# Weight scaling moved from GpSimd to ScalarE and batch 1 to 3 logits by 32-column matmuls, in a clustered attention and rational-activation MLP kernel

## The chip, the cores and the metric

One core of one Trainium2 chip runs the whole program. The metric is device time in microseconds of that core. Engine names are those of the profile: PE is TensorE (matmuls), PEld its weight loads, DVE VectorE, ACT ScalarE, POOL GpSimd, SP the queue that issues every data transfer.

## The reference, cut to what matters

```python
# q, k, v: (4, 8, 768, 64); centroids: (8, 16, 64)
q_assign = argmax(einsum('bhsd,hcd->bhsc', q_n, c_n), -1)   # q_n, k_n, c_n: rows of length 1
k_assign = argmax(einsum('bhsd,hcd->bhsc', k_n, c_n), -1)
mask = q_assign[..., :, None] == k_assign[..., None, :]
scores = where(mask, q @ k.T / 8, -1e9)
attn = softmax(scores) @ v
x = attn.transpose(0, 2, 1, 3).reshape(3072, 512)
h = x @ w_in                                                # w_in: (512, 2048)
P = a0 + a1*h + a2*h**2 + a3*h**3
Q = 1 + |b0|*|h| + |b1|*h**2
return (P / (Q + 1e-6)) @ w_out                             # w_out: (2048, 512)
```

Each row of q and of k is given to the cluster whose centroid has the largest inner product with it, its 16 **logits**; a query sees only the keys of its own cluster.

## The kernel before, in words

**Number format.** Operands of the large matmuls are split into two float16 parts, a high part and a low part (value minus high part), after a multiplication by a power of two. A product is three float16 matmuls (high by high, high by low, low by high) added up in PSUM.

**Weights** (`weights`, L660). `w_in` and `w_out` come in four chunks each. A chunk is four tiles of 128 x 512 that are loaded by SP, put together from 32-bit words by ACT and DVE (L701 and L708 are two DVE steps), and summed up so that a power of two follows (`wis` and `wos`). Then, for each of two pairs of tiles: one ACT operation over 1024 elements writes the high part as `scale * w` (the `act` call at L760; all ACT operations have the helper's line L546 in the profile); for each of the two tiles POOL multiplies the float32 words by the power of two in place (`tensor_scalar`, L777) and subtracts the high part from them, which gives the low part (`tensor_tensor`, L784). That is 16 ACT operations, 32 POOL multiplications and 32 POOL subtractions in all. The float32 words lie in a ring of 8 buffers (`big`) that raw loads and the MLP's intermediates use too.

**Attention.** Work goes by batch (4) and pair of heads (4 a batch). `prep` (L943) loads a pair's q, k and v, scales and splits them, turns them by transposing DMAs (PE in two pairs of batch 0), and then computes the logits of the pair's 2 x 768 queries and 2 x 768 keys into one tile `ptl` of 24 groups of 16. `logits` (L1154) does this with 48 matmuls (L1158), two for each group: the high part of the centroids starts a group's sum and their low part ends it, both with the same stationary operand and 16 columns. DVE takes the largest of each group (L1189), marks where it is reached (L1190, into `df`), and DVE and POOL make a mask of it that is appended to q and k before they are turned. Batch 0 then runs `attend_keys` (L1377); batches 1 to 3 run `attend` (L1255): 144 times, scores by four matmuls of 384 columns (L1277), minimum and scale on DVE (L1292), exponential and high part on ACT, low part on DVE (L1312), a transposing DMA, and the product with v (L1331).

**MLP** (`moe`, L1581). 12 blocks of 256 tokens: `x @ w_in` into tiles `ph` (L1639), the rational function on ACT, DVE and POOL, and the product with `w_out` into `po` (L1750).

**PSUM.** Eight banks in three rings: `m`, two single banks (`NM = 2`, used by `ph`, the attention outputs `px`, `ptl` and small things); `s`, two tiles of two banks each (the score tiles of `attend`); `o`, one tile of two banks (`po`).

**Order.** Every operation of every engine stands in a list written out by hand (`ORDER`, L31): 1001 entries for ACT, 1165 for DVE, 861 for PE, 640 for POOL, 384 for SP. A planner reads the lists, gives out buffers of the rings in that order and emits the program; semaphores follow from the data. An engine runs its list in sequence, so an entry that waits holds up all that stand behind it.

Of the kernel before, what the change touches and what calls it, by code (L numbers as in the profile page):

```python
# [27 lines left out]
K = {'ghd': 0.0, 'rvp': 0, 'look': 62.89, 'mulp': 0.4, 'sub': 0, 'xn': 14, 'NR': 8, 'sgp': 1, 'scp': 1, 'vsc': 0.75, 'sup0': 0, 'stk': 2, 'lop': 0, 'mgp': 0, 'rvn': 2, 'tq2': 2, 'at': 3, 'es': 4, 'vn': 2, 'ah': 5, 'rel': 0, 'twin': 1, 'pet': '_01', 'avs': 3, 'ksum': 1, 'fst': '_0', 'hpa': 1}  # L28
# [348 lines left out]
def clustered_attention_moe_kernel(  # L377
# [282 lines left out]
    def weights(name, i, vt):  # L660
# [91 lines left out]
        for m in range(2):  # L752
            hl = [whl[name, i, 2 * m + d] for d in range(2)]

            def hi(m=m):
                if name == "wi":
                    return win[i][:, 0, 2 * m : 2 * m + 2]
                return wout[i][:, 0, 2 * m : 2 * m + 2]

            act(  # L760
                ac(1024, 1), hi, lambda m=m: wp[m].ap.bitcast(F32), AF.Identity, [ws[2 * m], ws[2 * m + 1], ws_], hl, vt, [wp[m]],
                scale=sc,
            )
# [1105 lines left out]
```

## Time and profile before

| | |
|---|---|
| median of 3 runs | 896.92 us (894.39 to 898.39) |
| profiled execution, time | 897.27 us |
| profiled execution, span | 895.4 us |
| mean granted clock of PE | 0.994 |
| batch 0 attention and weights | about 0 to 205 us of the span |
| attention of batches 1 to 3 beside the MLP | about 179 to 760 us |
| MLP of the last batch alone | about 760 to 895 us |

Sums below are made against the profiled execution's 897.27 us; 1.9 us of it lie outside the span. The engines work side by side, so a busy time is not a share of the whole that could be added up with another's. A group of instructions has its busy time, the mean of one in ns, and behind the bar's end the idle time of its engine just before it and who ended that. PE's matmuls overlap in the records: two that start 25 ns apart are both shown with 169 ns.

### The profile page before, as it was taken

The page shows a single profiled execution, that of the slowest core. Times are in us where ns is not written, and L with a number is a line of the kernel's source. Part 1 is how long each engine was busy: PE and PEld are TensorE (multiplying, and loading weights), DVE is VectorE, ACT ScalarE, POOL GpSimd, SP SyncE. Part 2 cuts the span into 40 slices and gives each one's busy share as a digit, 9 for nine tenths or more (in the row PEclk, how much of TensorE's full clock was granted, in tenths as well). Part 3 has the DMA queues.
Part 4 walks back from the last instruction along what each step waited for, and adds up shares of the span by engine and source line. Part 5 has one row for each costly group of instructions (what it writes and reads, how often), then busy time and mean ns, then how long its engine had stood idle before and what let it go on. Part 6 is the DMA issues. An engine that isn't in the chain of part 4 may idle for free.

```text
span 895.4 us, 22725 instructions
## 1 busy us (share of the span) xinstructions
PE 849.1 (95%) x9045; PEld 597.8 (67%) x9045; DVE 785.8 (88%) x1388; ACT 755.2 (84%) x1050; POOL 629.3 (70%) x661
## 2 busy tenths in 40 slices
PE   2789999898999999999999999999999999999998
PEld 2557666675766777567776767777677666766664
DVE  7998979689989899999989998999889888876786
ACT  7557786899999989988999999998988898766674
POOL 1354685699988898778898988789988877422331
PEclk9899999999999999999999999999999999999999
DMA  8478755747989889999999799969888866300000
GB/s 278 138 170 198 190 161 144 206 96 145 194 166 217 159 163 213 188 191 197 167 220 175 154 186 179 180 133 214 144 159 126 160 126 113 87 1 25 7 25 25
DMA packets 364395, 134.70 MB, mean 150 GB/s; under 512 B 342144, under 2 KB 358528, under 8 KB 364288
## 3 DMA queue, kind: packets, MB, share of 16 engines
q1 hardware_dynamic: 364288, 133.24, 73.7%
q8 instruction: 71, 1.16, 0.5%
q14 instruction: 36, 0.29, 0.1%
HBM read 41.98 MB, written 6.29 MB: 54 GB/s over the span
## 4 chain that ended last, share of the span: by engine, by line
PE 55%; DVE 16%; ACT 11%; DMA 6%; issue 5%; POOL 5%; SPq 0%; ACTq 0%; DVEq 0%; POOLq 0%
PE po L1750 19%; PE ph L1639 17%; PE s L1277 6%; PE px L1331 5%; DVE top L1435 3%; ACT s L546 3%; DVE s L1292 3%; ACT u L546 2%; PE px L1506 2%; DVE ah L1312 2%; ACT ah L546 2%; PE z L1487 2%; DVE s L1732 1%; PE s L1408 1%; DMA rwi<-in_moe_w_in_dram 1%
## 5 line engine op out<-in xcount | busy, mean ns | idle before, releaser
L1639 PE MATMUL ph<-x,win 128*128 128x256 f16 x2304 | 267.6, 273 | 2.8 <-DVE xf L1357 1.2
L1750 PE MATMUL po<-wout,u 128*128 128x512 f16 x1152 | 268.6, 379 | 0.0
L1639 PEld LDWEIGHTS <-win 128*128 128x128 f16 x2304 | 223.2, 98 | 43.2 <-DVE xf L1357 3.5
L1679 POOL TENSOR_TENSOR s<-s,u 128x512 f32<-128x512 f32 x96 | 129.0, 1362 | 94.2 <-issue 52.6
L1750 PEld LDWEIGHTS <-u 128*128 128x128 f16 x1152 | 110.5, 98 | 115.3 <-issue 0.5
L1312 DVE SCALAR_TENSOR_TENSOR ah<-s,ah 128x768 f16<-128x768 f32 x144 | 136.1, 952 | 23.7 <-ACT ah L546 22.5
L1292 DVE TENSOR_SCALAR_CACHE_REDUCE s<-s,cc 128x768 f32<-128x768 f32 x144 | 145.2, 1019 | 9.3 <-PE s L1277 8.8
L546 ACT ACTIVATE s<-s,nm 128x768 f32<-128x768 f32 x144 | 125.4, 873 | 21.2 <-DVE s L1292 19.0
L1277 PE MATMUL s<-sk,sq 128*128 128x384 f16 x576 | 116.5, 329 | 4.1 <-DVE ah L1312 3.4
L546 ACT ACTIVATE ah<-s 128x768 f16<-128x768 f32 x144 | 115.9, 810 | 3.1
L1702 POOL TENSOR_TENSOR s<-s,u 128x512 f32<-128x512 f32 x72 | 102.0, 1429 | 16.9 <-ACT u L546 16.5
L1739 POOL TENSOR_TENSOR u<-s,u 128x512 f16<-128x512 f32 x72 | 86.4, 1207 | 30.9 <-DVE s L1732 14.5
L1331 PEld LDWEIGHTS <-at 128*128 128x128 f16 x2592 | 88.5, 98 | 13.6 <-issue 2.2
L1331 PE MATMUL px<-vhi,at 128*128 128x65 f16 x1728 | 91.1, 194 | 1.3 <-DMA at<-ah 0.8
L1331 PE MATMUL px<-vlo,at 128*128 128x64 f16 x864 | 86.8, 192 | 0.0
L1277 PEld LDWEIGHTS <-sq 128*128 128x128 f16 x576 | 52.9, 98 | 41.6 <-DVE ah L1312 8.7
L1660 DVE TENSOR_TENSOR t<-ph,t 128x512 f32<-128x512 f32 x96 | 65.4, 684 | 12.2 <-ACT t L546 11.7
L546 ACT ACTIVATE u<-ph 128x512 f32<-128x512 f32 x96 | 56.9, 595 | 21.8 <-PE ph L1639 21.3
L1732 DVE SCALAR_TENSOR_TENSOR s<-s,t 128x1024 f32<-128x1024 f32 (+1 forms) x49 | 63.0, 1286 | 1.4 <-POOL t L1716 0.6
L546 ACT ACTIVATE u<-t 128x1024 f16<-128x1024 f32 (+1 forms) x49 | 50.9, 1039 | 11.0 <-DVE t L1722 6.0
L546 ACT ACTIVATE t<-ph,gk 128x512 f32<-128x512 f32 x72 | 55.3, 774 | 0.0
L1665 DVE SCALAR_TENSOR_TENSOR t<-t,gk,ph 128x512 f32<-128x512 f32 x72 | 53.0, 742 | 1.1
(219 smaller groups left out, 1466.6 us busy)
## 6 DMA issues: line engine op xcount, KB each, us to landing
rwi<-in_moe_w_in_dram SPq DMA_DIRECT2D x16, 512.0 KB, 4.9
rwo<-in_moe_w_out_dram SPq DMA_DIRECT2D x16, 512.0 KB, 4.8
rk<-in_k_dram SPq DMA_DIRECT2D x32, 192.0 KB, 3.5
rq<-in_q_dram SPq DMA_DIRECT2D x32, 192.0 KB, 3.6
rvm<-in_v_dram SPq DMA_DIRECT2D x16, 384.0 KB, 4.1
rv<-in_v_dram SPq DMA_DIRECT2D x16, 384.0 KB, 4.6
out_dram<-ob SPq DMA_DIRECT2D x11, 512.0 KB, 3.8
at<-ah SPq DMA_TRANSPOSE x144, 4.1
```

The costliest lines, as they stand in the source:

```text
L546: lambda: nc.scalar.activation(out=out(), in_=in_(), func=func, **{a: (x() if callable(x) else x) for a, x in kw.items()}),
L1277: nc.tensor.matmul(sc.ap[:, i, :SH], lhsT=st["q" + x].ap[:, j, t, :], rhs=st["k" + x].ap[:, j, ks, :].rearrange("p t c -> p (t c)"), start ...
L1292: lambda nm=nm, view=view: ts(out=view(), in0=view(), scalar1=cc.ap, scalar2=None, op0=ALU.mult, op1=ALU.min, accum_out=nm.ap),
L1312: lambda part=part, view=view: stt(out=part(1), in0=view(), scalar=A_SCALE, in1=part(0), op0=ALU.mult, op1=ALU.subtract),
L1331: nc.tensor.matmul(px.ap[:, i, :w_], lhsT=at.ap[:, p_, kt, :], rhs=vv.ap[:, j, kt, :w_], start=(kt == 0 and vv is vhi and p_ == 0), stop=( ...
L1639: nc.tensor.matmul(ph[i].ap[:, fi * TW : (fi + 1) * TW], lhsT=win[f // 4][:, wpart, c, f % 4 * P : (f % 4 + 1) * P], rhs=xs[c].ap[:, xpart ...
L1660: lambda i=i, th=th, ph=ph: tt(out=th[i].ap, in0=ph[i].ap, in1=th[i].ap, op=ALU.mult),
L1679: lambda i=i, sh=sh, uh=uh: nc.gpsimd.tensor_tensor(out=sh[i].ap, in0=sh[i].ap, in1=uh[i].ap, op=ALU.mult),
L1702: lambda i=i, sh=sh, uh=uh: nc.gpsimd.tensor_tensor(out=sh[i].ap, in0=sh[i].ap, in1=uh[i].ap, op=ALU.mult),
L1732: lambda tw=tw, sw=sw: stt(out=sw(), in0=sw(), scalar=2.0, in1=tw(), op0=ALU.subtract, op1=ALU.mult),
L1739: lambda i=i, sh=sh, gl=gl, g16=g16, e=(nc.vector if gld else nc.gpsimd): e.tensor_tensor(out=gl[i].ap, in0=sh[i].ap, in1=g16()[:, 0, i * ...
L1750: nc.tensor.matmul(po[ti].ap, lhsT=g16()[:, part, c0 : c0 + P], rhs=wout[f // 4][:, wpart, f % 4], start=(k == 0 and f == f_first), stop=( ...
```

## The change

Three things. In `weights`, ACT multiplies the float32 words of a pair of tiles by the power of two in place (a new operation over 1024 elements), the high part is then a copy without a scale, and POOL's multiplications are not issued any more. In `prep` for batches 1 to 3, `ptl` is a two-bank tile of the ring `s` and not a single bank of `m`; a matmul takes both parts of the centroids as 32 columns, so that 24 matmuls write the two parts of each logit beside each other; an ACT copy takes the second part into `df` as float16, and a DVE addition puts the sum into PSUM, from where L1189 and L1190 read as before. Batch 0 keeps the 48 matmuls. `ORDER` is written anew for the new set of operations: 1029 entries for ACT, 1177 for DVE, 861 for PE, 608 for POOL, 384 for SP; in its lists most operations stand within a few places of where they stood. An option `lgw` that was off is removed. The helpers that the diff calls are in the kernel above; `K` gains `'lgb': '123', 'wsa': 1`.

```diff
...
@@ -757,9 +757,15 @@
                     return win[i][:, 0, 2 * m : 2 * m + 2]
                 return wout[i][:, 0, 2 * m : 2 * m + 2]
 
+            scaled = share("wsa", ((name == "wo") + 2 * i) * 2 + m)
+            if scaled:
+                act(
+                    ac(1024, 1), lambda m=m: wp[m].ap.bitcast(F32), lambda m=m: wp[m].ap.bitcast(F32), AF.Identity, [ws_],
+                    [ws[2 * m], ws[2 * m + 1]], vt, [wp[m]], scale=sc,
+                )
             act(
-                ac(1024, 1), hi, lambda m=m: wp[m].ap.bitcast(F32), AF.Identity, [ws[2 * m], ws[2 * m + 1], ws_], hl, vt, [wp[m]],
-                scale=sc,
+                ac(1024, not scaled), hi, lambda m=m: wp[m].ap.bitcast(F32), AF.Identity, [ws[2 * m], ws[2 * m + 1], ws_], hl, vt, [wp[m]],
+                **({} if scaled else {"scale": sc}),
             )
             for d in range(2):
                 c = 2 * m + d
@@ -772,13 +778,14 @@
                         [ws[c], ws_], [hl[d]], vt, [wp[m], ptok[m]], lock=True,
                     )
                 else:
-                    op(
-                        "POOL", pt1(512, 1),
-                        lambda c=c: nc.gpsimd.tensor_scalar(
-                            out=wf(c), in0=wf(c), scalar1=sc(), scalar2=0.0, op0=ALU.mult, op1=ALU.add
-                        ),
-                        [ws_], [ws[c]], vt, [wp[m]],
-                    )
+                    if not scaled:
+                        op(
+                            "POOL", pt1(512, 1),
+                            lambda c=c: nc.gpsimd.tensor_scalar(
+                                out=wf(c), in0=wf(c), scalar1=sc(), scalar2=0.0, op0=ALU.mult, op1=ALU.add
+                            ),
+                            [ws_], [ws[c]], vt, [wp[m]],
+                        )
                     op(
                         "POOL", pt2(512, True),
                         lambda c=c, h=hl[d]: nc.gpsimd.tensor_tensor(out=h.ap[:, 1], in0=wf(c), in1=h.ap[:, 0], op=ALU.subtract),
@@ -1137,23 +1144,31 @@
             turn(x, vt + kc("p2", b, 2), by_pe)
 
         G = 4 * NT
-        wide_ = bool(kn("lgw", 0))
-        ptl = misc([P, G, NCL], F32, f"ptl{n}") if not wide_ else None
-        if wide_:
-            halves = [misc([P, G // 2, 2, NCL], F32, f"ptl{x}{n}") for x in "qk"]
-
-            def wide_logits(i):
-                x = ("q1", "k1")[i]
-                for g in range(2):
-                    for t in range(NT):
-                        nc.tensor.matmul(
-                            halves[i].ap[:, g * NT + t], lhsT=st[x].ap[:, g, t, :], rhs=cen.ap[:, 0 : 2 + i : 1 + i, h0 + g, :],
-                            start=True, stop=True,
-                        )
+        paired = str(b) in kn("lgb", "")
+        if paired:
+            ptl = bank([P, 2, 512], F32, "s", f"ptl{n}", 2)
+        else:
+            ptl = misc([P, G, NCL], F32, f"ptl{n}")
+
+        def parts(i):
+            return ptl.ap[:, :, : G * NCL].rearrange("p x (g s c) -> p x g s c", s=2, c=NCL)[:, :, :, i]
+
+        def sums_():
+            return parts(0) if paired else ptl.ap.rearrange("p (x g) c -> p x g c", x=2)
+
+        def over_rows(a):
+            return a.rearrange("p (x g) c -> p x g c", x=2)
 
         def logits():
             for g, (x, part) in enumerate((("q1", 1), ("q1", 1), ("k1", 2), ("k1", 2))):
                 for t in range(NT):
+                    if paired:
+                        nc.tensor.matmul(
+                            ptl.ap[:, g // 2, (g % 2 * NT + t) * 2 * NCL : (g % 2 * NT + t + 1) * 2 * NCL].rearrange("p (s c) -> p s c", s=2),
+                            lhsT=st[x].ap[:, g % 2, t, :], rhs=cen.ap[:, 0 : part + 1 : part, h0 + g % 2, :],
+                            start=True, stop=True,
+                        )
+                        continue
                     for i in (0, part):
                         nc.tensor.matmul(
                             ptl.ap[:, g * NT + t, :], lhsT=st[x].ap[:, g % 2, t, :], rhs=cen.ap[:, i, h0 + g % 2, :],
@@ -1163,31 +1178,18 @@
         mx, mx2 = buf([P, G], F32, "mx", f"mx{n}", 1), buf([P, G], BF16, "mxi", f"mxi{n}", 1)
         df = buf([P, G, NCL], BF16, "df", f"df{n}", 1)
         oh = df
-        if wide_:
-            ptl = buf([P, G, NCL], F32, "lsm", f"lsm{n}", 1)
-            for i, x in enumerate(("q1", "k1")):
-                op("PE", 610, lambda i=i: wide_logits(i), [cen, st[x]], [halves[i]], vt + kc("p25", b, 2.5), [df, ptl], chain="logits" + x)
-                low = buf([P, G // 2, NCL], F32, "lsl", f"lsl{x}{n}", 2)
-                act(
-                    ac(192, 0, True), lambda low=low: low.ap, lambda i=i: halves[i].ap[:, :, 1], AF.Copy, [halves[i]], [low],
-                    vt + kc("p3", b, 3),
-                )
-                op(
-                    "DVE", 290,
-                    lambda i=i, low=low: tt(
-                        out=ptl.ap[:, i * 2 * NT : (i + 1) * 2 * NT], in0=halves[i].ap[:, :, 0], in1=low.ap, op=ALU.add
-                    ),
-                    [halves[i], low], [ptl], vt + kc("p3", b, 3), co=[ptl], lock=False,
-                )
-        else:
-            op("PE", 1205, logits, [cen, st["q1"], st["k1"]], [ptl], vt + kc("p25", b, 2.5), [df], chain="logits")
+        u = vt + kc("p25", b, 2.5)
+        op("PE", 645 if paired else 1205, logits, [cen, st["q1"], st["k1"]], [ptl], u, [df], chain="logits")
+        if paired:
+            act(ac(384, 0, True), lambda: over_rows(df.ap).bitcast(F16), lambda: parts(1), AF.Copy, [ptl], [df], u)
+            dve(465, lambda: tt(out=parts(0), in0=parts(0), in1=over_rows(df.ap).bitcast(F16), op=ALU.add), [df], [ptl], u)
 
         def spread(m):
             return m.ap.unsqueeze(2).broadcast_to([P, G, NCL])
 
         u = vt + kc("p3", b, 3)
-        dve(465, lambda: nc.vector.tensor_reduce(out=mx.ap, in_=ptl.ap, axis=AX.X, op=ALU.max), [ptl], [mx], u)
-        dve(463, lambda: tt(out=df.ap, in0=ptl.ap, in1=spread(mx), op=ALU.is_ge), [ptl, mx], [df], u)
+        dve(465, lambda: nc.vector.tensor_reduce(out=mx.ap.rearrange("p (x g) -> p x g", x=2), in_=sums_(), axis=AX.X, op=ALU.max), [ptl], [mx], u)
+        dve(463, lambda: tt(out=over_rows(df.ap), in0=sums_(), in1=over_rows(spread(mx)), op=ALU.is_ge), [ptl, mx], [df], u)
         op(
             *(("DVE", 465) if fast else ("POOL", 867)),
             lambda e=(nc.vector if fast else nc.gpsimd): e.tensor_tensor(
...
```

## Rows read from the trace of the kernel before

**Rows 1.** Page part 1: busy us (share of the span) xinstructions of each engine

```profile
PE 849.1 (95%) x9045; PEld 597.8 (67%) x9045; DVE 785.8 (88%) x1388; ACT 755.2 (84%) x1050; POOL 629.3 (70%) x661
```

**Rows 2.** Windows view, four stretches: busy time of each engine (instructions)

```profile
core 0: us, PE busy (x) PEld busy (x) DVE busy (x) ACT busy (x) POOL busy (x), PEclk, DMA share, GB/s
0.00:160.00 160.00, 131.84 (x1536) 95.01 (x1537) 142.72 (x322) 113.03 (x188) 82.63 (x119) 0.98 0.67 184
160.00:205.00 45.00, 38.73 (x510) 29.40 (x510) 34.69 (x77) 43.74 (x73) 37.12 (x51) 1.00 0.61 147
205.00:280.00 75.00, 73.22 (x759) 51.38 (x759) 67.95 (x113) 69.95 (x97) 67.21 (x65) 0.98 0.91 176
280.00:760.00 480.00, 474.28 (x5254) 334.96 (x5253) 440.01 (x758) 439.83 (x588) 404.71 (x399) 1.00 0.93 170
```

**Rows 3.** Chain of waits, stretch 280 to 760: shares by engine and line

```profile
by line: PE po L1750 18.3%; PE ph L1639 17.0%; PE s L1277 9.0%; PE px L1331 7.6%; issue 6.2%; ACT s L546 4.7%; ACT u L546 3.7%; DVE s L1292 3.3%; DVE ah L1312 2.9%; ACT ah L546 2.6%; DMA sk<-tk 2.3%; POOL s L1679 2.2%; DVE s L1732 2.0%; POO
```

**Rows 4.** PE in time order around one logits pass: start us, us, what

```profile
302.52 0.75 PE L1158 MATMUL ptl<-cen,sq 128*128 128x16 f16 x24
303.12 0.75 PE L1158 MATMUL ptl<-cen,sk 128*128 128x16 f16 x24
303.72 0.38 PE L1639 MATMUL ph<-x,win 128*128 128x256 f16 x2
```

**Rows 5.** Windows view of line L1158 alone: PE and PEld busy (instructions)

```profile
160.00:205.00 45.00, 2.71 (x96) 2.55 (x96) 1.00 0.61 147
205.00:280.00 75.00, 1.35 (x48) 1.35 (x48) 0.98 0.91 176
280.00:760.00 480.00, 12.15 (x432) 11.90 (x432) 1.00 0.93 170
```

**Rows 6.** Chain of waits, whole span: one attention-times-values piece, start us, us

```profile
298.41 1.65 PE px L1331 x54
```

**Rows 7.** Groups by line and form, ACT: PSUM reads and 1024-element operations

```profile
L546 ACT ACTIVATE rs<-px 128x256 f32<-128x256 f32 x12 | 4.5, 378 | 0.2 <-PE px L1549 0.2
L546 ACT ACTIVATE u<-ph 128x512 f32<-128x512 f32 x96 | 56.9, 595 | 21.8 <-PE ph L1639 21.3
L546 ACT ACTIVATE u<-t 128x1024 f16<-128x1024 f32 x47 | 49.7, 1057 | 9.4 <-DVE t L1722 4.4 <-DVE s L1695 2.7 <-POOL s L1702 1.3
L546 ACT ACTIVATE wout<-wwo,wos 128x1024 f16<-128x1024 f32 x8 | 9.0, 1141 | 1.7 <-DVE wos L641 1.7
```

**Rows 8.** Groups by line: the second DVE read of the logits

```profile
L1190 DVE TENSOR_TENSOR df<-ptl,mx 128x384 bf16<-128x384 f32 x16 | 8.9, 555 | 0.3
```

**Rows 9.** Line L546 on ACT, 150 to 180: high parts, duration ns min/median/max, first and last start

```profile
L546 ACT ACTIVATE win<-wwi,wis x2: 1155/1156/1156, 152.7 to 153.7; 128x1024 f16<-128x1024 f32 x2
L546 ACT ACTIVATE wout<-wwo,wos x2: 1136/1142/1149, 175.1 to 178.0; 128x1024 f16<-128x1024 f32 x2
```

**Rows 10.** Windows view of line L777 alone: POOL busy (instructions)

```profile
0.00:160.00 160.00, 22.10 (x25) 0.98 0.67 184
160.00:205.00 45.00, 4.79 (x7) 1.00 0.61 147
```

**Rows 11.** Line L777 on POOL: duration ns min/median/max; then a wait

```profile
L777 POOL TENSOR_SCALAR wwi<-wwi,wis x16: 687/692/1650, 34.0 to 174.2; 128x512 f32<-128x512 f32 x16
...
  ACT win L546: 13.5, 5
```

**Rows 12.** Groups by line: one step of weight assembly on DVE, both matrices

```profile
L701 DVE SCALAR_TENSOR_TENSOR wwo<-rwo,wwo 128x512 int32<-128x512 int32 x16 | 12.9, 808 | 0.1
L701 DVE SCALAR_TENSOR_TENSOR wwi<-rwi,wwi 128x512 int32<-128x512 int32 x16 | 10.8, 686 | 0.1
```

**Rows 13.** DVE in time order: the last read of the pass in rows 4

```profile
305.19 0.56 DVE L1190 TENSOR_TENSOR df<-ptl,mx 128x384 bf16<-128x384 f32 x1
```

**Rows 14.** Line L1277 on PE (scores): what ended its idle time, us, times

```profile
  DVE ah L1312: 12.1, 22
```

**Rows 15.** Line L1639 on PE: what ended its idle time, us, times

```profile
  DVE df L1190: 1.5, 2
```

More of the change, by code (lines that the diff above doesn't have):

```diff
@@ L25 @@
 M_BIG, M_MID, M_LOW = 2.0 ** 15, 2.0 ** 7, 2.0 ** -4
-K = {'ghd': 0.0, 'rvp': 0, 'look': 62.89, 'mulp': 0.4, 'sub': 0, 'xn': 14, 'NR': 8, 'sgp': 1, 'scp': 1, 'vsc': 0.75, 'sup0': 0, 'stk': 2, 'lop': 0, 'mgp': 0, 'rvn': 2, 'tq2': 2, 'at': 3, 'es': 4, 'vn': 2, 'ah': 5, 'rel': 0, 'twin': 1, 'pet': '_01', 'avs': 3, 'ksum': 1, 'fst': '_0', 'hpa': 1}
+K = {'ghd': 0.0, 'rvp': 0, 'look': 62.89, 'mulp': 0.4, 'sub': 0, 'xn': 14, 'NR': 8, 'sgp': 1, 'scp': 1, 'vsc': 0.75, 'sup0': 0, 'stk': 2, 'lop': 0, 'mgp': 0, 'rvn': 2, 'tq2': 2, 'at': 3, 'es': 4, 'vn': 2, 'ah': 5, 'rel': 0, 'twin': 1, 'pet': '_01', 'avs': 3, 'ksum': 1, 'fst': '_0', 'hpa': 1, 'lgb': '123', 'wsa': 1}
 ORDER = {
     "ACT": """
[32 rows of a table removed]
[33 rows of a table added]
 """,
     "DVE": """
[37 rows of a table removed]
[37 rows of a table added]
 """,
     "PE": """
[28 rows of a table removed]
[28 rows of a table added]
 """,
     "POOL": """
[21 rows of a table removed]
[20 rows of a table added]
 """,
     "SP": """
[13 rows of a table removed]
[13 rows of a table added]
 """,
```

262 rows, old and new, of the table ORDER are left out of this document.

## The prediction

> **What bounds the kernel now.** I began with the page's busy shares: PE is busy for 95% of the span, DVE for 88%, ACT for 84%, POOL for 70% [rows 1]. An average over stages says little, so the next view was the windows, cut where the work changes [rows 2]. There the reader is to see three regimes. Up to 160 us (batch 0 and the weights) DVE is the fullest, with 142.7 of 160 us; PE has 28 us idle and ACT 47. From 160 to 205 us ACT is full: 43.7 of 45 us, while PE and DVE are idle for 6 and 10. From 280 to 760 us (attention of batches 1 to 3 beside the MLP) PE is idle for 5.7 of 480 us; DVE, ACT and POOL are idle for 40, 40 and 75. The last regime is the longest, so the chain of waits was read for it alone: the four large PE lines, L1750, L1639, L1277 and L1331, make 18.3 + 17.0 + 9.0 + 7.6 = 51.9% of it [rows 3]. So PE is full there, but the chain leaves it for ACT, DVE and DMA about every second microsecond: a view that bears on a rival below.
>
> **The logits matmuls.** One pass of 48 matmuls starts at 302.52 and the next PE work starts at 303.72 [rows 4]: 1.20 us, or 25.0 ns for each of 48 matmuls of 16 columns. After the change a pass has 24 of 32 columns. No row has 32 columns, so I bound one from both sides: 25.0 ns as with 16, and 1.65 us / 54 = 30.6 ns as with 64 and 65 [rows 6]. A pass then takes 0.60 to 0.73 us. I take 0.60, because 32 is nearer to 16 and the weight load that goes with each matmul stays as it is. The saving is 0.60 us a pass (0.47 at the least). The passes lie so: 432 matmuls, which is nine passes, from 280 to 760 us, one pass from 205 to 280, two from 160 to 205 [rows 5]; these are the twelve of batches 1 to 3. Where ACT is full, two passes bring nothing; from 205 us on PE is full and ten bring 10 x 0.60 = **6.0 us** (4.7 at the least price; 3.1 if only the chain's PE share counts).
>
> The Trainium skill, "TensorE: Matmul & The Clock Gate", section "Wait — 56ns, not 53.3ns?", says that matmuls never start closer than about 25 ns, and gives 25 ns for 32 columns too. By that figure a pass would be an estimated 24 x 25 = 0.60 us and the sum the same; the trace agrees for 16 columns, with 25.0 ns, and no run yet shows it for 32.
>
> **The two operations that come with them.** An ACT copy of 384 elements from PSUM lies between 378 ns (256 elements) and 595 ns (512) [rows 7]; I take the middle, 0.49 us. The DVE addition has the form of L1190, 384 elements with one input from PSUM: 0.56 us [rows 8]. For twelve pairs ACT gets 5.8 us and DVE 6.7, nine pairs of them where both are idle for 40 us each. The mask is prepared ahead of the pair that uses it, and the idle time covers them, but not wholly. In that stretch the chain's ACT pieces shown add up to 4.7 + 3.7 + 2.6 = 11.0% and the DVE ones to 3.3 + 2.9 + 2.0 = 8.2% [rows 3], so 9 x 0.49 x 0.11 + 9 x 0.56 x 0.08 = **0.9 us** is put on the path. The ends are 0 and, with the cover gone, 9 x 1.05 = 9.5 us.
>
> **The weights on ACT.** A pair of weight tiles costs ACT one operation of 1.14 us now; after it, one of that kind and one without a scale, for which the nearest row is the 1024-element ACT operation with float16 output at 1.06 us [rows 7]. That is 1.06 us more for each of 16 pairs, 17 us in all. Fourteen pairs come before 160 us, where ACT has 47 us idle and 14.8 are wanted: nothing, with up to 14.8 if the cover is gone. The last two start at 175.1 and 178.0 us [rows 9], where ACT is full: 2 x 1.06 = **2.1 us** on the path, the upper end 4.2 with the two pairs at 152.7 us that stand right ahead of the full stretch, the lower end 0 if the new lists bring other ACT work across 205 us.
>
> **The weights off POOL.** 32 multiplications go, 22.1 + 4.8 = 26.9 us busy [rows 10]. POOL is idle for 77 us before 160, so its own time counts for nothing there. What counts is DVE, the fullest: a POOL multiplication takes from 687 to 1650 ns for the same work [rows 11], 26.9 - 32 x 0.69 = 4.8 us in all above its median, so POOL and DVE hold each other up in places. On DVE's side the same step of the assembly takes 808 ns for one matrix and 686 for the other [rows 12]: 16 x 0.12 = **2.0 us** off DVE, between 0 (it was another POOL operation) and 4.8.
>
> No DMA is added or taken away, and SP's list keeps its 384 entries. What stands behind the new ACT operations is the high part and, behind it, POOL's subtraction, which must wait for both as it waits for the high part now; POOL waits for that 13.5 us in 5 places [rows 11], so the low parts can't come earlier than ACT allows.
>
> **The sum.** -6.0 + 0.9 + 2.1 - 2.0 = -5.0 us against the profiled execution's own 897.27 us: 892.3. That execution stands 0.35 us over the median of 896.92, so I say **892.0 us**.
>
> **Rivals.**
> 1. *The logits wait in the scores' place.* `ptl` now sits in one of two score tiles. Today's pass holds its bank from 302.52 to 305.19 + 0.56 = 305.75 us [rows 4, 13], 3.2 us; with 0.6 less for PE and 1.05 more for the copy and the addition it holds a score tile for 3.7 us, hand-overs not counted. PE has already waited for score tiles 22 times, 12.1 us in all [rows 14], so they are scarce. If each pass puts off the scores behind it by half its hold, twelve put them off by 22 us; PE's list has MLP work to fill this. With half of it filled 11 us stay: 892.3 + 11 = 903 us, slower. It decides once over 5/22, about a quarter, of the delay isn't filled. Against it: the rewritten lists can place MLP entries there, and the MLP's ring gets a bank back, for which PE waited only 1.5 us in 2 places [rows 15].
> 2. *PE's fullness is only apparent.* Its records overlap [rows 4]. The saving then counts by PE's share of the chain, 0.519 x 6.0 = 3.1: 897.27 - 3.1 + 0.9 + 2.1 - 2.0 = 895.2 us, no change. The Trainium skill, "Perfetto Trace Analysis", section "Identifying the Most-Contended Engine", speaks for this rival: it calls matmul busy time a bad measure and asks for the weight loads' share. By rows 2 that share is 335 of 480 us, 70%, not 98.8%. For PE speaks that the pass of rows 4 and the MLP work behind it follow each other without a gap: the saved time is time that PE's list really takes.
> 3. *ACT pays in full at the end of batch 0*, 4.2 us and no relief for DVE: 897.27 - 6.0 + 0.9 + 4.2 = 896.4 us, no change.
> 4. *Relief for DVE is at its upper end*, 4.8 us in the stretch that DVE bounds: 889.5 us.
>
> **How the numbers follow.** A measurement of this kernel can tell about 0.5%, 4.5 us, from no change. My sum gets 0.40, of which 0.28 lie more than 4.5 us below (its copies and additions are the loosest term), 0.12 within. Rival 1 gets 0.18: scarce tiles are shown, but not that PE lacks other work. Rival 2 gets 0.17, rival 3 0.10, rival 4 0.15. Faster 0.28 + 0.15 = 0.43; the same 0.12 + 0.17 + 0.10 = 0.39; slower 0.18. The range goes from 884 (rival 4 and some 5 us more for the rewritten lists, whose effect no row prices) to 904 (just past rival 1's price); outside are the worse half of rival 1, 0.09, and about as much below and beyond. The likeliest case's own range is 888 to 896.
>
> **What would show it.** Right: 24 L1158-type matmuls a pass at 25 ns; the stretch that was 280 to 760 us about 5 us shorter with PE still idle for some 6 us; POOL without its 26.9 us; the shared DVE step at 690 ns for both matrices; the stage before the last batch's attention ending within 2 us of where it did. Wrong: waits of PE's scores on DVE's logits readers, or a total above 12.1 us on score tiles (rival 1); PE's idle time in the long stretch up by as much as its work fell (rival 2); a stretch with ACT full that ends 4 us later (rival 3).

## The result and the profile after

The change makes the kernel slower: 905.92 us median (903.73 to 909.92) against 896.01, a ratio of 1.0113 (95% interval 1.0084 to 1.0142). The prediction said 892.0 us, range 884 to 904. The profiled execution took 903.73 us, 6.6 us of span more than the one of before, and these 6.6 us are what the two traces can place.

Page part 1 of the changed kernel (busy us, share of the span, instructions) and its chain of waits by engine:

```profile
PE 843.1 (93%) x8757; PEld 587.8 (65%) x8757; DVE 794.7 (88%) x1400; ACT 772.5 (86%) x1078; POOL 603.4 (67%) x629
...
PE 46%; DVE 21%; ACT 16%; issue 8%; DMA 4%; POOL 4%; SPq 1%; DVEq 0%; POOLq 0%; ACTq 0%
```

Against [rows 1] PE has 6.0 us less work, ACT 17.3 more, DVE 8.9 more, POOL 25.9 less. The work moved as the diff says; the time did not follow it. PE's share of the chain is 46%; the same line of before says 55%.

The windows view, cut as in [rows 2]:

```profile
0.00:160.00 160.00, 128.81 (x1526) 92.50 (x1526) 140.43 (x318) 122.26 (x199) 62.00 (x96) 0.99 0.68 184
160.00:205.00 45.00, 38.99 (x473) 28.73 (x470) 33.78 (x74) 43.80 (x74) 29.57 (x40) 1.00 0.62 141
205.00:280.00 75.00, 72.22 (x731) 50.55 (x732) 68.25 (x119) 73.58 (x104) 68.55 (x67) 0.98 0.94 179
280.00:760.00 480.00, 465.68 (x4985) 323.52 (x4983) 446.33 (x763) 438.83 (x591) 403.31 (x398) 1.00 0.90 168
```

In the long stretch PE is idle for 14.3 us where it was idle for 5.7. In a window of fixed length less work is always more idle time, so this says little by itself; the stretch from the first scores of batch 1 to the last holds the same attention work in both kernels. Before and after:

```profile
179.10:759.80 580.70, 569.14 (x6265) 402.88 (x6262) 529.45 (x908) 534.95 (x723) 496.30 (x491) 1.00 0.91 168
```

```profile
181.90:766.30 584.40, 565.06 (x5993) 394.73 (x5991) 540.38 (x922) 540.51 (x735) 493.80 (x487) 1.00 0.89 166
```

There PE's work falls by 4.1 us and its idle time rises by 7.8, from 11.6 to 19.3. Up to 160 us PE got 3.0 us less done than before.

The scores' line of the changed kernel: instances, duration, first and last start, then what PE waited for ahead of it (us, times). Below it, the same first row of before.

```profile
L1279 PEld LDWEIGHTS <-sq x576: 94/98/152, 181.9 to 766.3; 128*128 128x128 f16 x192
...
  DVE ah L1314: 23.4, 38
  issue: 6.5, 12
  DVE df L1192: 1.7, 4
```

```profile
L1277 PEld LDWEIGHTS <-sq x576: 95/98/151, 179.1 to 759.8; 128*128 128x128 f16 x192
```

The first scores of batch 1 come 2.8 us late, the last scores 6.5 us late, and the MLP behind them takes as long as before. So 2.8 us were lost up to the first scores and 3.7 in the stretch of the scores, 584.4 us long instead of 580.7. PE's waits for score tiles (those that end with DVE's low part, L1314) doubled from 12.1 us [rows 14] to 23.4, but only 1.7 us of waits name the logits' own reader, L1192.

One logits pass of the changed kernel, PE, ACT and DVE in time order (start us, us):

```profile
386.41 0.46 PE L1166 MATMUL ptl<-cen,sq 128*128 128x32 f16 x12
386.71 0.45 PE L1166 MATMUL ptl<-cen,sk 128*128 128x32 f16 x12
387.01 1.46 PE L1752 MATMUL po<-wout,u 128*128 128x512 f16 x6
387.20 0.49 ACT L546 ACTIVATE df<-ptl 128x384 f16<-128x384 f32 x1 [0.62 <-PE ptl L1166]
388.14 0.55 DVE L1185 TENSOR_TENSOR ptl<-ptl,df 128x384 f32<-128x384 f32 x1
388.73 0.56 DVE L1191 TENSOR_REDUCE mx<-ptl 128x24 f32<-128x384 f32 x1
389.31 0.56 DVE L1192 TENSOR_TENSOR df<-ptl,mx 128x384 bf16<-128x384 f32 x1
389.93 0.44 PEld L1279 LDWEIGHTS <-sq 128*128 128x128 f16 x4 [0.43 <-DVE df L1192]
```

The prices that the prediction gave the logits part are met here: 24 matmuls of 32 columns take 0.60 us (386.41 to 387.01), the copy 0.49, the addition 0.55, and the score tile is held from 386.41 to 389.87, 3.5 us. The rows also show what no price held: ACT stood for 0.62 us waiting for the pass, and the next scores waited 0.43 us until L1192 had read the logits for the last time, which frees their score tile.

### The profile page after: what moved, and what is told of

Its sections match the earlier page's. It is cut to its first block, busy times and chain, and to the rows that moved or that the text cites. A ratio compares the mean times of both kernels' runs of the same rounds, so it can differ in the third digit from the quotient of the medians.

```text
span 902.0 us, 22145 instructions
## 1 busy us (share of the span) xinstructions
PE 843.1 (93%) x8757; PEld 587.8 (65%) x8757; DVE 794.7 (88%) x1400; ACT 772.5 (86%) x1078; POOL 603.4 (67%) x629
## 4 chain that ended last, share of the span: by engine, by line
PE 46%; DVE 21%; ACT 16%; issue 8%; DMA 4%; POOL 4%; SPq 1%; DVEq 0%; POOLq 0%; ACTq 0%
PE ph L1641 18%; PE po L1752 16%; PE s L1279 5%; PE px L1333 4%; ACT s L546 4%; DVE top L1437 4%; DVE s L1294 3%; ACT u L546 3%; ACT ah L546 3%; DVE ah L1314 2%; DMA sq<-tq 2%; DVE s L1734 2%; POOL s L1681 1%; DVE t L1724 1%; DMA rwo<-in_moe_w_out_dram 1%
## 5 line engine op out<-in xcount | busy, mean ns | idle before, releaser
L1314 DVE SCALAR_TENSOR_TENSOR ah<-s,ah 128x768 f16<-128x768 f32 x144 | 136.0, 951 | 23.3 <-ACT ah L546 22.3
L546 ACT ACTIVATE s<-s,nm 128x768 f32<-128x768 f32 x144 | 125.4, 873 | 18.3 <-DVE s L1294 16.4
L1279 PE MATMUL s<-sk,sq 128*128 128x384 f16 x576 | 115.7, 328 | 10.7 <-DVE ah L1314 8.7
L546 ACT ACTIVATE ah<-s 128x768 f16<-128x768 f32 x144 | 115.9, 810 | 3.0
L546 ACT ACTIVATE u<-ph 128x512 f32<-128x512 f32 x96 | 56.6, 595 | 20.8 <-PE ph L1641 20.6
L546 ACT ACTIVATE u<-t 128x1024 f16<-128x1024 f32 (+1 forms) x49 | 50.8, 1038 | 10.1 <-DVE s L1697 6.9
L546 ACT ACTIVATE t<-ph,gk 128x512 f32<-128x512 f32 x72 | 54.9, 772 | 0.0
```

What stands on the lines that cost most here:

```text
L546: lambda: nc.scalar.activation(out=out(), in_=in_(), func=func, **{a: (x() if callable(x) else x) for a, x in kw.items()}),
L1279: nc.tensor.matmul(sc.ap[:, i, :SH], lhsT=st["q" + x].ap[:, j, t, :], rhs=st["k" + x].ap[:, j, ks, :].rearrange("p t c -> p (t c)"), start ...
L1314: lambda part=part, view=view: stt(out=part(1), in0=view(), scalar=A_SCALE, in1=part(0), op0=ALU.mult, op1=ALU.subtract),
```

## The experiments

Two theories stood at the start. **Parts**: the operations that were added cost what the change lost. **Lists**: the rewritten `ORDER` lists lose it, since every engine runs its list in sequence and the lists of before fit each other on the chip. All ratios are to runs of the kernel before on the same chip; edits are cut to the lines that matter. "Fitted" lists were rearranged until the planner's own costs rated them like the lists of before.

**The changed kernel with one part taken back** (its lists kept, entries left out or put in; in e2 17 more entries move by one or two places, so that the lists run through).

```diff
 # e1_pool_scale: POOL multiplies again
-'lgb': '123', 'wsa': 1
+'lgb': '123', 'wsa': 0
 # e2_narrow_m: 48 narrow matmuls again, bank of ring m
-'lgb': '123', 'wsa': 1
+'lgb': '', 'wsa': 1
 # e3_narrow_s: as e2, with the tile in the score ring
-ptl = misc([P, G, NCL], F32, f"ptl{n}")
+ptl = bank([P, G, NCL], F32, "s", f"ptl{n}", 2) if str(b) in "123" else misc([P, G, NCL], F32, f"ptl{n}")
```

> The changed kernel with one part undone: POOL multiplies the weights again (32 multiplications back, each just ahead of its subtraction; 16 ACT operations out); the logits stay as changed and all lists keep their sequence. Theory ACT (the multiplications on ACT cost 3 us, as the first scores of batch 1 start at 182.0 us against 179.1): 903 us, first scores back near 179. Theory tiles (the loss comes from the logits in a score tile, between 280 and 760 us): 904 to 906 us, the loss after 280 us unchanged. Theory lists (the rewritten lists are worse in themselves): 906 us. If relief of POOL was worth 2 us, 908 us.

> The changed kernel with the other part undone: batches 1 to 3 compute their logits by 48 matmuls into a single bank of ring m again, without the copy and the addition; the weights stay on ACT; the lists keep their sequence but for 17 entries that had to move by one or two places to run through. Theory tiles: 906 - 7 = 899 us, PE idle in the long stretch back from 14 to about 6 us. Theory that PE's time alone counts: 906 + 6 = 912 us. Theory lists: 906 us or more.

> The changed kernel with 48 narrow matmuls and no copy and no addition, but with the logits still in a score tile; the lists keep their sequence with no entry moved. It parts the place from the two new operations. Theory tiles in its plain form (the place alone costs it): 905 to 910 us, with PE 6 us fuller and its waits for score tiles still over 20 us. Theory operations (the copy and the addition, in line behind other work of ACT and DVE, are what keeps the tile): 899 to 902 us, with the waits near 12 us.

Measured: 911.74 us (ratio 1.0150, 1.0127 to 1.0173), 930.54 (1.0374, 1.0349 to 1.0399) and 910.30 (1.0156, 1.0135 to 1.0177). None is faster than the changed kernel (1.0113), also where an extra operation went out (e3 has neither copy nor addition): e2 is clearly slower, e1 and e3 by some 0.4%, at the edge of what the intervals can tell. So the parts can't be priced by taking them out of lists written for them, and the theory of the parts alone falls.

**The weights part alone on the lists of before**, twice. In e4 ACT's new entry stands right ahead of the high part, 8 other entries had to move, and 5 buffers of the float32 ring went to other users. In e11 no entry moved and every buffer went to its old users: the planner reckons with the old lengths, and one load is handed its buffer behind an ACT entry, as it was before.

```diff
 # e4_act_scale_old_lists, e11_act_scale_old_lists_old_buffers
+act(..., [ws_], [ws[2 * m], ws[2 * m + 1]], vt, [wp[m]], scale=sc)
-op("POOL", pt1(512, 1), ...)
 # e11 only, in slot_time()
+if o.seq == 1197 and self.ops[282] not in order:
+    return None
```

> The kernel before with the weights part alone: each ACT multiplication stands right ahead of its high part in the old list, POOL's 32 are out, 8 entries moved by one to three places to run through; the logits as before. Theory ACT: 896 + 3 = 899 us, first scores of batch 1 near 182 us. Theory tiles says nothing of this part: 896. My prediction's step for this part: 896 + 0.1 us. Theory lists: 896 or less.

> The weights part alone on the old lists: ACT multiplies right ahead of each high part, POOL's multiplications are out, no other entry moved, and every buffer of every ring goes to the same users in the same order as before. The run of the same part before it (911 us) had 8 entries moved and 5 buffers of the float32 ring handed out otherwise, and lost its 12 us between 160 and 205 us. If ACT's extra 17 us are what was paid there: 908 to 912 again, first scores of batch 1 some 12 us late. If it was the handout of the buffers: 893 to 898, first scores within 3 us of before. My sum for this part alone: 2.1 more on ACT and 2.0 less on DVE, 896 to 897.

Measured: 911.22 us (1.0163, 1.0145 to 1.0180) and 904.24 (1.0080, 1.0061 to 1.0098). The windows of e11 up to 160 and to 205 us:

```profile
0.00:160.00 160.00, 126.62 (x1507) 90.38 (x1508) 139.07 (x314) 121.05 (x194) 62.91 (x92) 0.99 0.64 177
160.00:205.00 45.00, 38.51 (x476) 30.01 (x477) 30.48 (x74) 43.63 (x74) 27.06 (x40) 1.00 0.57 155
```

With sequence and buffers kept, the part as a whole (ACT's operations in, POOL's out) costs about 7 us. The profiled execution is the longest of the six, 10.7 us of span over the one of before: its first scores of batch 1 come 4.8 us late, its last 10.7. So some half of its loss lies ahead of the first scores. It was looked for between 160 and 205 us, but there PE does what it did (38.5 us against 38.7); up to 160 us it gets 5.2 us less done than in [rows 2], although ACT, with 8.0 us more work, is still idle for 39. The other half is lost in the stretch of the scores. What holds PE in either place is not isolated. The 7 us between e11 and e4 are moved entries and other buffers.

**Old operations, new lists, and each part with fitted lists.**

```diff
 # e5_old_ops_new_lists: K of before, ORDER fitted from the changed kernel's lists
 # e6_act_scale_fitted: the weights part alone, ORDER fitted from the lists of before
 # e7_wide_logits_fitted: the logits part alone, ORDER fitted from the changed kernel's lists
 # e8_both_fitted_more: the whole change, ORDER fitted further
-ORDER = {...}
+ORDER = {...}
```

> The control. The operations of the kernel before (POOL multiplies, 48 narrow matmuls in ring m), in lists that descend from the changed kernel's and were searched anew by the planner's rules, as the two given kernels' lists were, until they fit these operations as well as the old lists do by the planner's own measure. Nothing of the change is in it but the ancestry of its lists. If the lists of such a search differ among themselves on the chip by as much as the loss, this is 903 to 908 us (theory lists). If the operations make the loss (theories tiles and ACT), this is 894 to 899 us.

> The weights part alone (ACT multiplies, POOL's 32 are out; old logits), with lists that start from the old ones and were searched anew until they fit as well as the old lists do. Theory ACT: 896 + 3 = 899 us, with the loss before 205 us. My prediction's step: 896 us. Theory lists: 903 to 908 us, as any list but the old one.

> The logits part alone (32-column matmuls into a score tile, copy and addition; POOL multiplies), with lists that start from the changed kernel's and were searched anew until they fit as well. Theory tiles: 896 + 4 to 7 = 900 to 903 us, with waits for score tiles over 18 us and the loss between 280 and 760 us. My prediction's step: 896 - 5 = 891 us. Theory lists: 903 to 908 us.

> The changed kernel's operations, all of them, with its lists searched for longer by the same rules, so that they fit better than the given ones. Theory tiles and ACT: the operations cost what they cost, 900 to 906 us. Theory lists, if a longer search helps on the chip: 895 to 900 us; if a search cannot see what the chip does, 903 to 908 us as the others.

Measured: 915.34 us (1.0216, 1.0192 to 1.0240), 905.73 (1.0108, 1.0086 to 1.0131), 915.59 (1.0216, 1.0193 to 1.0238), 916.87 (1.0239, 1.0216 to 1.0263). e5 is the control: not one operation differs from before, and it loses 19 us, twice what the change lost. The planner's costs can't tell these lists apart; the chip can. Its lists are a third set, though, neither those of before nor the changed kernel's, so it shows how much lists can cost and not what the changed kernel's own cost. The score-tile waits grow in e6 too, which has no change of the logits:

```profile
  DVE ah L1314: 19.5, 33
```

**The logits part on the lists of before.** First the matmuls alone: 24 a pass, still of 16 columns and into the old bank, with the centroids' low part left out.

```diff
 # e9_24_matmuls_old_lists
-for i in (0, part):
+for i in (0, part) if b == 0 else (0,):
```

> The kernel before, with its own lists and its own buffers, not one entry moved; batches 1 to 3 issue only the 24 logits matmuls with the high part of the centroids (their low part is left out), into the same bank, with no copy and no addition. It prices the matmuls alone. If PE's list is what sets the long stretch, as the prediction's sum says: 0.60 us for each of ten passes, 6 us less, about 890 us. If PE's fullness is only apparent (rival 2): 0 to 3 us less, 893 to 896. If the time of this kernel answers to any change of an operation's length by some us either way, because every list then meets the others elsewhere: anything up to 905, and the stretch from 280 to 760 us would show no saving.

Measured: 898.58 us (1.0005, 0.9988 to 1.0022). Half the matmuls are gone, and nothing is gained. PE in time order around one pass, before and in e9 (whose profiled execution is its longest, 903.13 us):

```profile
360.52 0.75 PE L1158 MATMUL ptl<-cen,sq 128*128 128x16 f16 x24
361.13 0.74 PE L1158 MATMUL ptl<-cen,sk 128*128 128x16 f16 x24
361.73 0.82 PE L1277 MATMUL s<-sk,sq 128*128 128x384 f16 x4
```

```profile
360.70 0.45 PE L1173 MATMUL ptl<-cen,sq 128*128 128x16 f16 x12
361.00 0.45 PE L1173 MATMUL ptl<-cen,sk 128*128 128x16 f16 x12
361.90 0.82 PE L1279 MATMUL s<-sk,sq 128*128 128x384 f16 x4 [0.46 <-DVE ah L1314]
```

Before, the pass and the scores follow without a gap, which is what the prediction read as "PE is full". In e9 the pass is 0.6 us shorter and the scores start 1.20 us after it began, just as they did before: they wait for DVE to free a score tile. Of the twelve passes of e9 this is the only one where the wait comes at once. Behind the other eleven the next entry starts 0.61 us after the pass began, so PE did go on sooner; the time is lost further on. The pass of [rows 4] is one of them. Behind it stand the MLP's matmuls and then scores, before and in e9:

```profile
303.72 4.09 PE L1639 MATMUL ph<-x,win 128*128 128x256 f16 x36
307.65 0.81 PE L1277 MATMUL s<-sk,sq 128*128 128x384 f16 x4
```

```profile
302.68 0.45 PE L1173 MATMUL ptl<-cen,sq 128*128 128x16 f16 x12
303.29 4.16 PE L1641 MATMUL ph<-x,win 128*128 128x256 f16 x36
307.74 0.81 PE L1279 MATMUL s<-sk,sq 128*128 128x384 f16 x4 [0.28 <-DVE ah L1314]
```

The scores start 5.13 us after the pass before, 5.06 in e9, now with a wait for a score tile that was not there; the next pass starts 58.00 us after this one before and 58.02 in e9. DVE's low part that frees the tile starts 4.04 us after the pass in both (L1312 at 306.56, L1314 at 306.72): it came no sooner, and PE's saving lasted until PE needed the tile. Over the whole run PE waits 17.5 us for score tiles in e9, against 12.1 before.

Then the copy and the addition, one by one, with every old entry and buffer in its place, and a control that only swaps neighbours at the same 24 places.

```diff
 # e10_24_matmuls_copy_add_old_lists; e15_24_matmuls_copy_only without the second line
+act(1, lambda: over_rows(df.ap).bitcast(F16), lambda: sums_(), AF.Copy, [ptl], [df], u)
+dve(1, lambda: tt(out=sums_(), in0=sums_(), in1=over_rows(df.ap).bitcast(F16), op=ALU.add), [df], [ptl], u)
 # e16_24_swapped_neighbours: 12 swaps such as this in ACT's list, 12 in DVE's
-1303 860
+860 1303
```

> As the run with 24 matmuls on the old lists, with the same buffers, and with the two operations that the change adds for each of twelve pairs: an ACT copy of 384 elements from PSUM to float16, put behind the ACT entry that was running when the pass ended, and a DVE addition ahead of the maximum (what they add is the high part again, so each logit is doubled). Beside that run it prices the two operations. My sum: 0.9 us more than it. With the cover gone: 9.5 us more. If it is the copy standing in ACT's list (an entry that waits for PE and holds up the exponentials behind it) that costs: 3 to 9 us more, with PE's waits for score tiles above the 12 us of before.

> As the run with 24 matmuls, the copy and the addition on the old lists (911.0), but the addition is left out: it prices the copy alone. If the copy's place in ACT's list is what costs (each exponential behind it is late by 0.48 us and by the wait for PE): 907 to 911. If the addition on DVE costs: 898 to 902. If both cost by their time on engines that are nearly full: half, 904 to 905.

> The kernel before, its operations and its buffers; only, at each of the twelve places in ACT's list and the twelve in DVE's where the run with copy and addition has its new entries, two neighbouring entries have changed places. Nothing is added or left out. If these lists answer to any disturbance there: 903 to 912. If only added work and new waits cost: within 2 us of before, 896 to 900.

Measured: e10 911.00 us (1.0156, 1.0135 to 1.0177), e15 905.20 (1.0093, 1.0075 to 1.0111), e16 905.96 (1.0113, 1.0093 to 1.0134). Against e9 the copy costs 0.9%, some 8 us, and the addition 0.6% more: together about 13 us, beside 12.6 us of added work (12 x 0.49 and 12 x 0.56). It looks as if nothing hid them, but e16 forbids that reading: no work added, 24 pairs of neighbours exchanged at the same places, and the time rises by 9 us, as much as the whole change cost. How much of the 13 us is the operations' own time and how much the disturbance is not separated. The windows of e16:

```profile
205.00:280.00 75.00, 71.21 (x742) 49.93 (x743) 68.55 (x116) 69.81 (x97) 65.72 (x66) 0.98 0.87 174
280.00:760.00 480.00, 468.69 (x5193) 329.74 (x5192) 433.60 (x748) 433.52 (x579) 398.96 (x393) 1.00 0.93 168
```

Same work, 5.6 us more idle time on PE than [rows 2] in the long stretch, 6.4 more on DVE, 6.3 more on ACT: all three lose together, and the windows name no single engine that sets the pace. It is one choice of 24 swaps; others were not tried.

The whole logits part on the old lists needed 64 moved entries, so that the lists run through with the tile in the score ring:

```diff
 # e12_wide_logits_old_lists
-'lgb': '', 'wsa': 0
+'lgb': '123', 'wsa': 0
```

> The logits part alone on the old lists: 24 matmuls of 32 columns into a tile of the score ring, the copy and the addition; 64 entries are moved, as few as let the lists run through with the tile in that ring, and POOL multiplies the weights as before. Lists newly fitted gave 915.6 for this part. If the fitted lists were to blame and the score tiles are not scarce: 890 to 893. If the score tiles are the cost (rival 1, 11 us on the sum): 902 to 906, with PE's waits for score tiles at 20 us or more against 12. If the price is in the lists however few entries move: above 900 without more waits for score tiles.

Measured: 949.77 us (1.0574, 1.0557 to 1.0591), some 51 us slower. What PE waited for ahead of the scores (us, times):

```profile
  DVE df L1193: 53.2, 17
  DVE ah L1315: 15.8, 28
```

L1193 is the last read of the logits (L1192 in the changed kernel), which frees the score tile that they lie in. These waits and those for the other users of the score tiles add up to 69.0 us, 56.9 more than the 12.1 of before, and the span is 56.1 us longer. So here the logits' hold of a score tile, rival 1's mechanism, accounts for the loss; what the 64 moved entries add to it is not separated. In the changed kernel's lists the same wait comes to 1.7 us.

**What takes the place of PE's saved time.** The transposing transfers (DMA share 0.93 in [rows 2]) and the loop through the score tiles were the candidates. e13 transfers only the high half of each exponential tile and reads it twice in the product with v; e14 is e13 with the 24 matmuls; e17 is e13 with DVE's low part cut from 768 to 128 columns; e18 is e17 with the 24 matmuls.

```diff
 # e13_half_transposes, e14_half_transposes_24_matmuls
-out=at.ap.rearrange("p s k c -> p (s k) c"), in_=ah.ap.rearrange("p s k -> p (s k)"),
+out=at.ap[:, 0], in_=ah.ap[:, 0],
-lhsT=at.ap[:, p_, kt, :]
+lhsT=at.ap[:, 0, kt, :]
 # e17_short_low_part, e18_short_low_part_24_matmuls
-out=part(1), in0=view(), scalar=A_SCALE, in1=part(0),
+out=part(1)[:, :, :64], in0=view()[:, :, :64], scalar=A_SCALE, in1=part(0)[:, :, :64],
```

> The kernel before, its lists and buffers, with one thing left out: the 144 transposing transfers of the exponentials in batches 1 to 3 carry only the high half, and the product with v reads the high half where it read the low one, so PE's, DVE's, ACT's and POOL's work stays the same. If the transfers, busy for 0.93 of the long stretch, are what sets its pace beside PE: 10 us or more less, below 888, with the DMA share well down and PE's idle time in that stretch below the 5.7 us of before. If they are hidden behind PE and the score tiles: within 3 us of before, 895 to 901, with a DMA share near 0.6.

> As the run with half transposes, and with the 24 logits matmuls a pass of the earlier run (the centroids' low part left out). If the full transfers were what swallowed PE's saved time: 5 to 6 us less than the run with half transposes alone. If the score tiles, and so DVE and ACT, swallow it: no difference beyond 2 us from that run, and PE's waits for score tiles grow by as much as its work falls.

> The run with half transposes, whose low part nobody reads, and in it DVE computes the low part of the exponentials for 128 of 768 columns only: 144 operations of 0.95 us become some 0.2 us each, and each score tile comes free some 0.7 us sooner. Lists and buffers are those of before, PE's work is unchanged. If the loop through the score tiles holds PE back: PE's idle time in the long stretch falls from 5 us to under 2 and the whole is 4 to 9 us shorter, 887 to 892. If PE is full by its own list and nothing else matters there: within 2 us of 896.

> As the run with the short low part, with the 24 logits matmuls a pass. If the loop swallowed PE's saved time, the saving shows now that the loop is short: 4 to 7 us less than that run, 10 passes at 0.60 us. If something else swallows it (the ACT part of the loop, the MLP's ring): less than 2 us less than that run.

Measured: e13 896.14 us (0.9989, 0.9973 to 1.0006), e14 896.92 (1.0006, 0.9992 to 1.0021), e17 888.41 (0.9908, 0.9894 to 0.9922), e18 888.75 (0.9910, 0.9894 to 0.9926). The long stretch of e13 and of e14, and the stretch from 280 to 745 us of e17 and then of e18 (last lines of their windows views, sums only):

```profile
280.00:760.00 480.00, 475.10 (x5289) 335.65 (x5287) 441.15 (x758) 440.55 (x590) 405.51 (x400) 1.00 0.64 120
280.00:760.00 480.00, 470.01 (x5033) 328.74 (x5032) 440.22 (x756) 438.49 (x589) 403.81 (x399) 1.00 0.64 119
```

```profile
sum 465.00, PE 462.10 PEld 328.60 DVE 368.59 ACT 429.23 POOL 403.42; mean PE 462.10 PEld 328.60 DVE 368.59 ACT 429.23 POOL 403.42
```

```profile
sum 465.00, PE 459.19 PEld 323.37 DVE 370.32 ACT 430.29 POOL 404.43; mean PE 459.19 PEld 323.37 DVE 370.32 ACT 430.29 POOL 404.43
```

The DMA theory falls: the share goes from 0.93 to 0.64 and the time stays. The score-tile loop is half right. In e14 PE has 5.1 us less work than in e13 and 5.1 us more idle time in the same total time, and it waits 16.5 us for score tiles instead of 12.1. With DVE's part shorter (e17) it waits 3.5 us for them, and the kernel is 0.9% faster than before. But the 24 matmuls bring nothing there either: PE idles 2.9 us in e17 and 5.8 in e18, and ACT, at 92% in both, does not move. The expectation that the saving would show once the loop is short was wrong. Three pairs of runs agree: ten passes shortened by 0.60 us are worth 0 here, to within some 2 us. What paces e18 is not isolated.

## Why the prediction was wrong, point by point

**-6.0 us for the matmuls: the first step that failed.** The price of a pass, 0.60 us, was right to the hundredth; the step from "from 205 us on PE is full" to ten times that price on the total was not. Rival 2 named the mechanism, PE's fullness only apparent, and its 3.1 us were still too many: e9, e14 and e18 show 0 us, and e9's interval ends at a gain of 1.1. The prediction held against rival 2 that the pass and the work behind it follow without a gap. That reading was right at the place, as the next entry did start sooner behind eleven of twelve passes, and the conclusion was wrong: the saving was gone when PE next needed a score tile, since DVE's work came no sooner. The evidence was in [rows 3]: a chain that leaves PE every second microsecond says that PE's entries often wait for other engines' work.

The Trainium skill, "Perfetto Trace Analysis", section "Identifying the Most-Contended Engine", says that matmul busy time is no measure of PE's headroom. The trace agrees: PE was shown busy for 99% of the long stretch of e13, and in e14 5.1 us less of its work became 5.1 us of idle time.

**+0.9 us for copy and addition: mis-sized.** On the lists of before, with every old entry in its place, they cost about 13 us (e10 against e9), beyond even the upper end of 9.5 that was kept for the cover gone. Weighting by the chain's shares (11% and 8%) was the error: idle time of 40 us on each engine need not lie where the entry stands, and e16 shows that a disturbance at these places costs 9 us even without added work.

**+2.1 us for the weights on ACT and -2.0 for DVE: mis-sized together.** The sum held 0.1 us for this part; e11 measures about +7. About half of the loss in its profiled execution lies ahead of the first scores, nearly all of that before 160 us, in the stretch of the fourteen pairs that I put at nothing because ACT was idle for 47 us there; the rest comes in the stretch of the scores. The relief for DVE did not come in the changed kernel: the step at L701 was to take 690 ns for both matrices and takes 761 and 773, and the three lines of the assembly, L696, L701 and L708, took 13.14 + 23.64 + 22.96 = 59.7 us before and take 15.08 + 24.38 + 22.56 = 62.0 after. Why is not shown.

**The rewritten lists: the step left without a price.** I let them count for some 5 us on the good side of the range only. e5 shows 19 us on the bad side with the same operations in other lists, e16 9 us for 24 exchanged neighbours. Such a term is larger than any that the sum held. How large it is in the changed kernel's own lists no run isolates.

**The rivals.** Rival 1 gave 903 us, near the result, and that nearness is luck. Its mechanism is real, as e12's 53.2 us show, but the changed kernel's lists keep it down to 1.7 us. Its other sign, waits above 12.1 us on score tiles, came and could not tell it from rival 2: e9, with the logits in their old bank, has 17.5 us, e6, with the old logits, 19.5, and e2, with the logits moved back out of the score tiles in the changed kernel's lists, 25.2. Whether the hold adds to the changed kernel's 23.4 us by a detour is not shown. Rival 2's sign, idle time up by as much as the work fell, holds in any window of fixed length and shows nothing there; e14 beside e13 does show it, as the total stays the same. Rival 3 (896.4) and rival 4 (889.5) both count the matmuls' 6.0 us, which are worth nothing, and e11 rules out their prices for the weights.

**What stays open.** On the lists of before the parts together cost far more than the change did (e11 about 7 us, and e10 about 13 without the move to the score ring, e12 some 51 with it). The changed kernel's own lists avoid e12's waits; beyond that, its 10 us can't be divided between operations and lists. Whether lists fitted on the chip would bring the change below the kernel before was not tried. No version with the whole computation was faster than the kernel before.

## What to carry to other kernels

Where several engines are all above 85% busy and run fixed lists, a saving on one lasts only until it next waits for another: follow it past the next entry, which may well start sooner, to the next entry that another engine releases, and look at that and not at the busy share. Before pricing a change that also rewrites the order, run the old operations in a slightly disturbed order; here 24 exchanged neighbours cost as much as the change itself, so any sum of a few us was below what the order alone does. An operation put into such a list is not free because its engine is idle on average: price it by a run with the old order around it. And add up everything that released an engine ahead of a line: in e12, the slowest run, the usual releaser shows 15.8 us of waits and another one 53.2.

## What the runs showed of the hardware that was not expected

The 16 DMA engines at a share of 0.93 were no bound: with transposes of half the size (landing in 2.9 us instead of 4.1) the share fell to 0.64 and the time did not change. The Trainium skill, "Perfetto Trace Analysis", section "Identifying the Most-Contended Engine", calls occupancy misleading for DMA; these runs agree.

PE's clock fell after a stall and stayed low behind it. Three windows of e4, 165 to 180 us:

```profile
165.00:170.00 5.00, 4.84 (x81) 4.08 (x79) 1.21 (x5) 4.56 (x8) 0.00 (x0) 1.00 1.10 294
170.00:175.00 5.00, 0.57 (x6) 0.26 (x3) 2.47 (x5) 2.48 (x6) 0.00 (x0) 0.76 0.39 140
175.00:180.00 5.00, 3.57 (x28) 2.75 (x30) 3.77 (x11) 3.59 (x7) 3.41 (x8) 0.56 0.73 203
```

PE, at the full 2.4 GHz up to 170 us, then did 0.57 us of work in 5; the mean granted clock fell to 0.76 and, in the next window with PE back at 3.57 us of work, to 0.56, which is mostly the lower level of 1.2 GHz. Sixteen matmuls of the same form in e4, at full clock and behind the stall:

```profile
151.44 1.08 PE L722 MATMUL wig<-wwi 128*128 128x128 bf16 x16
176.43 1.89 PE L722 MATMUL wog<-wwo 128*128 128x128 bf16 x16 [5.86 <-DVE rs L1559]
```

From 176.4 to 178.3 us the windows view gives a granted clock of 0.50. The work behind the stall took 1.89 us instead of 1.08, so this stall cost more than its own length.
